# Four experts on one core: GpSimd's second parts of weights in pieces of 256 elements, and weight blocks split at other places of the program

## The chip, the core and the metric

The kernel runs on one core of a Trainium2 chip. The metric is the device time of one execution in microseconds (us). It was measured in three runs; one more execution was recorded by the hardware profiler, and all rows below come from that one.

The engines go by these names: PE multiplies matrices (TensorE; PEld is its loading of weights), DVE is VectorE, ACT is ScalarE, POOL is GpSimd, SP starts DMAs. SBUF is the memory on the chip, PSUM holds what PE writes. L1030 is line 1030 of the kernel before.

## What is computed

Attention over 2 x 8 heads (576 positions, a bias computed from distances), then a feed-forward layer with a rational activation, then a mixture of four experts. All is float32. The change lies in the experts alone:

```python
def _moe2_ref(x, domain_probs, w1, w2):      # x 1152 x 512, w1 4 x 512 x 1024, w2 4 x 1024 x 512
    p = domain_probs / (domain_probs.sum(-1, keepdims=True) + 1e-09)
    out = np.zeros((N, D), dtype=np.float32)
    for e in range(E):
        h = np.maximum(x @ w1[e], 0.0)
        out += p[:, e:e + 1] * (h @ w2[e])
    return out
```

## The kernel before

**Two parts per number.** PE multiplies float32 operands as a first part (the number rounded, made by an ACT copy) and a second part (number minus first part, made by a subtraction on DVE or POOL); each product is three matmuls: first x first, first x second, second x first. Activations are split as they come out of PSUM. Weights are loaded by SP into one of two `stage` buffers and split from there. A *split* below is ACT's copy followed by the subtraction.

**Two ways through the experts.** The 1152 tokens are three chunks of 384. One chunk goes the plain way, expert after expert (`expert_first`, four blocks f2 of first weights; then `expert_second`, three tiles t of 128 tokens, which need all four blocks of second weights). This is the *single part*; it ends at 531.66 us. The other two chunks, T1 and T2, then go together, again expert after expert: the *paired part*. There the two chunks and the two halves of the 512 inputs make a 2x2 block matrix, multiplied with 7 products in place of 8. For each of four groups g of an expert (`Square(e, g)`), product m (1 to 7) is 6 matmuls of 384 columns into one of three PSUM banks (`sa` for m = 1, 2; `sb` for 6, 5, 3; `sc` for 7, 4), and `gather(m)` has DVE and ACT add the products up in `part_sums`:

- m = 6: L1041 reads `sb` (after that m = 5 may add to it); m = 5: L1045 reads `sb` (after that m = 3 may), L1046 reads `sc`; m = 3: L1049; m = 4: L1052.
- Each finished quarter of h goes to `parts`: L1029 (ACT, first part with ReLU) and L1030 (DVE, second part). Three of four of these take h from `part_sums`, so both inputs of L1030 are in SBUF; the fourth takes it from `sa`, in PSUM.

The products run in this order: `(1 6 7 2 5)` of group 0, then for g = 1 to 3: `(1 6)` of g, `(3 4)` of g-1, `(7 2 5)` of g. That makes 26 products up to the last `5` of group 3, which I number 0 to 25; product 20 is m = 6 of group 3, product 21 is m = 3 of group 2. Then six tiles of `op` (`tile_products`) multiply h with the second weights. I call the 26 products the *squares* of an expert.

**Weights of the paired part.** A `Group` (G0 to G3 of each expert) holds one group's blocks `b` and their combinations `s`. It takes five steps: 0, ACT copies `b` (L400, L401); 1, DVE or POOL makes their second parts (L403, L404); 2, POOL makes the combinations in place in `stage` (L406 to L409, one after the other); 3, ACT copies them (L411); 4, DVE or POOL makes their second parts (L413). m = 1 needs steps 0 and 1, m = 6 needs all five. The second weights T0 to T3 (`WT`) are split in one step (L369, L370), on POOL.

**What sets the order.** Each engine works through its instructions in the order in which they are written. `order` lists the weight blocks in the order of their splitting; `turns(n)` does the next n steps of that list at its place in the program, and does nothing when the buffers' last readers are not yet written; `load_ahead` starts the load of the next block but one when a block is done. `side[0]` says who makes second parts of groups: DVE in the single part and beside the tiles, POOL beside the squares. `LAST_TURNS` and `TURNS` are the tables of places. `first` takes one of two PSUM buffers `hp`, so the product after next waits for ACT's L839 and DVE's L840 to have read it.

Of the kernel before, what the change touches and what calls it, by code (L numbers as in the profile page):

```python
# [15 lines left out]
ALU = mybir.AluOpType  # L16
# [5 lines left out]
E, FE = 4, 1024  # L22
# [25 lines left out]
def attention_then_two_ffn(ctx: ExitStack, tc: tile.TileContext, q, k, v, w1, b1, w2, w_in, w_out, ca, cb, probs, e_w1, e_w2, c_l, c_l8, c_p, c_x, out):  # L48
    nc = tc.nc
    act, dve, pool, pe, sp = nc.scalar, nc.vector, nc.gpsimd, nc.tensor, nc.sync  # L50

    def f32(ap):
        return ap.bitcast(F32)
# [119 lines left out]
    def catch_up(calls):  # L173
        now, calls[:] = calls[:], []
        for f in now:
            f()
# [150 lines left out]
    class Piece:  # L327
# [39 lines left out]
        def split(self):  # L367
            t = self.w.t[:, self.rows]
            act.activation(t[:, :, 0, :], self.raw, AF.Copy)  # L369
            self.w.eng.tensor_tensor(t[:, :, 1, :], self.raw, f32(t[:, :, 0, :]), ALU.subtract)  # L370

    class Group:
# [22 lines left out]
        def work(self, step, eng):  # L395

            b, s, raw = self.b, self.s, self.raw
            b11, b12, b21, b22 = (raw[:, i] for i in range(4))
            if step == 0:
                act.activation(b[:, 0, 0], b11, AF.Copy)  # L400
                act.activation(b[:, 2:4, 0], raw[:, 2:4], AF.Copy)  # L401
            if step == 1:
                eng.tensor_tensor(b[:, 0, 1], b11, f32(b[:, 0, 0]), ALU.subtract)  # L403
                eng.tensor_tensor(b[:, 2:4, 1], raw[:, 2:4], f32(b[:, 2:4, 0]), ALU.subtract)  # L404
            if step == 2:
                pool.tensor_tensor(b11, b12, b11, ALU.subtract)  # L406
                pool.tensor_tensor(b12, b22, b12, ALU.subtract)
                pool.tensor_tensor(b22, b22, b11, ALU.subtract)
                pool.tensor_tensor(b21, b21, b22, ALU.subtract)  # L409
            if step == 3:  # L410
                act.activation(s[:, :, 0], raw, AF.Copy)  # L411
            if step == 4:
                eng.tensor_tensor(s[:, :, 1], raw, f32(s[:, :, 0]), ALU.subtract)  # L413

    W1 = [(Weight(w_in, f2, False), Weight(w_out, f2, True)) for f2 in range(DFF // 256)]
    W2 = [[(Weight(e_w1[e], f2, False, 1), Weight(e_w2[e], f2, True, 1)) for f2 in range(FE // 256)] for e in range(E)]
# [1 line left out]
    order = [W1[f2][second] for grp in GROUPS for second in range(2) for f2 in grp]  # L418
    for e in range(E):
        order += [p[0] for p in W2[e]] + [p[1] for p in W2[e]]  # L420
    WS = [[Group(e_w1[e], g) for g in range(4)] for e in range(E)]
    WT = [[Weight(e_w2[e], f2, True, 1, pool) for f2 in range(FE // 256)] for e in range(E)]
    for e in range(E):
        order += WS[e][:3] + WT[e][:2] + WS[e][3:] + WT[e][2:]
    S_SLOT, T_SLOT = W_SLOT[3:5], W_SLOT[5]
    WO = W_SLOT * 3 + W_SLOT[:3] + (W_SLOT[6:] + W_SLOT[:3]) * E

# [11 lines left out]
    def can_convert():  # L439

        if state["done"] == len(order):
            return False
        return all(x not in holder or holder[x].left == 0 for x in order[state["done"]].slots())

    def convert(steps=5):

        for _ in range(steps):
            if state["step"] == 0 and not can_convert():
                return
            i = state["done"]  # L450
            if isinstance(order[i], Group):
                if state["step"] == 0:
                    order[i].place()
                order[i].work(state["step"], side[0])
                state["step"] = (state["step"] + 1) % 5
                if state["step"] == 0:
                    under_way.pop(i)
                    state["done"] += 1
                    load_ahead()
            elif state["step"] < 4:  # L460
                under_way[i].narrow(state["step"])
                state["step"] += 1
            else:
                order[i].place()
                under_way.pop(i).split()
                state["step"] = 0
                state["done"] += 1
                load_ahead()
# [224 lines left out]
    for i in range(-2, len(units)):  # L693
        if i + 2 < len(units):
            n, u = units[i + 2]
# [5 lines left out]
        if 0 <= i + 1 < len(units):  # L701
            n, u = units[i + 1]
            pair[n].exp(u)
        if i >= 0:
            n, u = units[i]
# [3 lines left out]
    def ready(w):  # L709
        while state["done"] <= order.index(w):  # L710
            assert state["step"] or can_convert()
            convert(5 - state["step"])
        return w.t
# [122 lines left out]
    def expert_first(u, f2):  # L836
        h = first(W2[u][f2][0], CHUNKS[0])
        hi, lo = tmp("h_hi", F32R), tmp("h_lo", F32R)
        act.activation(hi, h, AF.Relu)  # L839
        dve.scalar_tensor_tensor(out=lo, in0=h, scalar=0.0, in1=f32(hi), op0=ALU.max, op1=ALU.subtract)  # L840
        h_of[u, f2] = hi, lo
# [3 lines left out]
    for i in range(1, len(units) + LAG):  # L845
        on = i < len(units)
        if on:
            c, f2 = units[i]
# [70 lines left out]
    def turns(n):  # L919

        for _ in range(n):
            if state["done"] < len(order) and state["step"] == 0 and isinstance(order[state["done"]], Weight) and can_convert():
                state["step"] = 4
            convert(1)
# [28 lines left out]
    for i, a in enumerate((acc_01[:, 0], acc_01[:, 1], acc_2[:, 0])):  # L953
        acc_of[CHN // P * CHUNKS[0] + i] = a

    LAST_TURNS = 1, 1, 2, 3, 2, 3
    for u in range(E):
        for f2 in range(1, 4):
            if (u, f2) != (0, 1):
                expert_first(u, f2)  # L960
            turns(LAST_TURNS[f2 - 1] if u == E - 1 else 2 - f2 // 2 + ((u, f2) == (0, 2)))
            if 0 < u < E - 1 and results:
                results.pop(0)()
        if u + 1 < E:
            expert_first(u + 1, 0)
        for t in range(3):
            expert_second(u, t)
            if (u, t) == (E - 2, 0):
                assert not results
                making = sums_of_x()  # L970
            if (u, t) in ((E - 2, 0), (E - 1, 0), (E - 1, 1)):
                next(making)
            turns(LAST_TURNS[3 + t] if u == E - 1 else 1 + (t == 2))

    ffn.close()
    psum.close()
# [2 lines left out]
    def bank(tag):  # L979
        return ps.tile([P, 512], F32, tag=tag, name=tag)  # L980
# [12 lines left out]
    class Square:  # L993
# [13 lines left out]
        def __call__(self, *which):  # L1007

            for m in which:
                if m == 1:  # L1010
                    self.begin()
                k, x = RIGHT[m], LEFT[m]
                bank = self.bank[{1: 0, 2: 0, 3: 1, 5: 1, 6: 1, 4: 2, 7: 2}[m]]
                i = 0
                for c in range(2):
                    for wpart, xpart in ((0, 0), (0, 1), (1, 0)):
                        pe.matmul(bank, lhsT=self.w.t[k[0]][:, k[1], wpart, c], rhs=x[c][:, xpart], start=i == 0 and m in (1, 6, 7), stop=i == 5, skip_group_check=True)  # L1017
                        i += 1
                if m == 4:
                    self.w.left = 0  # L1020
                side[0] = pool
                waiting = self.gather(m)
                catch_up(later)
                later.extend(waiting)
                turns((self.g, m) in TURNS[self.e > 0])

        def parts(self, v, t):
            def f():
# [24 lines left out]
                return self.parts(u2, h21)  # L1053
            return []

    TURNS = [(0, 1), (0, 6), (0, 5), (1, 1), (1, 6), (0, 4), (1, 7), (1, 2), (1, 5), (1, 4), (2, 7), (2, 5), (3, 5)], [(0, 6), (0, 5), (0, 4), (1, 7), (1, 2), (1, 3), (1, 4), (2, 5), (3, 5)]
    for e in range(E):
        sq = [Square(e, g) for g in range(4)]
        sq[0](1, 6, 7, 2, 5)
        for g in range(1, 4):  # L1060
            sq[g](1, 6)
            sq[g - 1](3, 4)
            sq[g](7, 2, 5)

        tiles = [(c, t) for c in (T1, T2) for t in range(3)]
        ops = {}

        def tile_products(k, fs, begin, end):
            c, t = tiles[k]
            if begin:  # L1070
                ops[k] = bank("op")
            for x in (WT[e][f // 2] for f in fs):
                ready(x)
            j = CHN // P * c + t
            halves = (slice(0, DM),) if (e, k) != (E - 1, 5) else (slice(0, DM // 2), slice(DM // 2, DM))
            for cols in halves:
                second_products(ops[k][:, cols], lambda f, part: hs[f, c][:, part, t * P:(t + 1) * P], WT[e], fs, begin, end, cols)
                if end:
                    catch_up(later)
                    gathered(e, j, ops[k][:, cols], cols)  # L1080

        SOON, LATE = (0, 4, 1, 5, 2, 6), (3, 7)
        tile_products(0, SOON, True, False)
        sq[3](3, 4)
        catch_up(later)
        tile_products(1, SOON, True, False)
        for k in range(6):
            tile_products(k, LATE if k < 2 else SOON + LATE, k > 1, True)
            if k == 5:
                for x in WT[e]:  # L1090
                    x.left = 0
            side[0] = dve
            turns(2 if k < 2 else 3)


# [40 lines left out]
```

## Time and profile before

| | us |
|---|---|
| runs: median of 3 (lowest, highest) | 813.6 (811.23, 815.51) |
| profiled execution, its own time | 815.37 |
| its span, first to last instruction | 813.5 |
| PE busy | 771.0 (95% of the span) |
| DVE busy | 568.0 (70%) |
| ACT busy | 427.4 (53%) |
| POOL busy | 251.7 (31%) |
| paired part, 531.66 to the end | 281.9 |

The busy shares are means over stages. The single part keeps PE busy without a gap from 425 to 531.66 us; the gaps of the paired part lie in the squares. In timeline rows, `x6` merges six instructions, and what stands in brackets is the engine's idle time ahead of the row and who ended it. "PEclk" is the clock that was granted to TensorE, as a share of its full speed.

### The profile page before, as it was taken

How to read it: one execution, taken by the hardware profiler on the slowest of the kernel's cores; microseconds unless marked ns; L12 is line 12 of the kernel's file. 1: busy time of each engine (PE TensorE's matmuls, PEld its weight loads, DVE VectorE, ACT ScalarE, POOL GpSimd, SP SyncE). 2: the span in 40 equal slices, each digit the busy share in tenths (PEclk: the TensorE clock that was granted, in tenths of full speed). 3: DMA queues.
4: the chain of work that ended last, by engine and by line, in shares of the span. 5: the costliest groups of instructions: out<-in, count | busy, mean ns of one | idle time of the engine just before them, and what ended most of it. 6: DMA issues, size and time to landing. Idle time of an engine off the chain costs nothing.

```text
span 813.5 us, 15824 instructions
## 1 busy us (share of the span) xinstructions
PE 771.0 (95%) x6470; PEld 664.6 (82%) x6470; DVE 568.0 (70%) x868; ACT 427.4 (53%) x689; POOL 251.7 (31%) x207
## 2 busy tenths in 40 slices
PE   8998999988999999999999999987998998899898
PEld 5445666657999999999999898887887888888787
DVE  7989789996999999998754465457437436643831
ACT  6987567655988888787533352425224213322410
POOL 0000225432445466431100000166246145334510
PEclk9999999999999999999999999999999999999999
DMA  8898685640332133311143352223022112212101
GB/s 151 191 227 191 144 212 117 145 112 2 104 104 105 56 100 103 104 38 67 53 130 128 106 164 100 69 95 104 27 69 89 51 52 79 76 28 78 52 27 52
DMA packets 83945, 79.41 MB, mean 98 GB/s; under 512 B 38016, under 2 KB 62976, under 8 KB 83200
## 3 DMA queue, kind: packets, MB, share of 16 engines
q1 hardware_dynamic: 83440, 78.39, 35.2%
q8 instruction: 51, 0.84, 0.4%
q14 instruction: 22, 0.18, 0.1%
q10 hardware_dynamic: 432, 0.01, 0.0%
HBM read 59.20 MB, written 2.36 MB: 76 GB/s over the span
## 4 chain that ended last, share of the span: by engine, by line
PE 43%; DVE 24%; issue 11%; POOL 10%; ACT 8%; DMA 3%; SPq 1%; POOLq 0%; DVEq 0%; ACTq 0%
PE op L56 15%; PE hp L56 10%; PE sc L56 4%; PE o L568 4%; DVE hid L221 3%; DVE narrow L365 2%; DVE narrow L363 2%; DVE h L1030 2%; DVE qd L758 2%; PE yp L56 2%; PE sb L1017 2%; POOL w L370 2%; PE sc L1017 2%; DVE u L759 2%; DMA stage<-in_moe_w_dram 2%
## 5 line engine op out<-in xcount | busy, mean ns | idle before, releaser
L56 PE MATMUL hp<-x,wi 128*128 128x384 f32 x888 | 159.6, 337 | 2.8 <-DVE u L769 2.5
L56 PEld LDWEIGHTS hp<-x,wi 128*128 128x128 f32 x888 | 153.9, 188 | 5.6 <-issue 2.6
L56 PE MATMUL op<-w,h 128*128 128x512 f32 (+1 forms) x600 | 133.1, 382 | 0.6 <-DVE acc L888 0.6
L56 PEld LDWEIGHTS op<-w,h 128*128 128x128 f32 x600 | 109.5, 188 | 22.4 <-DVE acc L888 0.8
L56 PE MATMUL yp<-g_hi,w 128*128 128x384 f32 x384 | 102.1, 336 | 0.4 <-ACT y L824 0.4
L888 DVE SCALAR_TENSOR_TENSOR acc<-op,pr_sb,acc 128x512 f32<-128x512 f32 (+1 forms) x28 | 20.5, 731 | 82.3 <-PE op L56 82.3
L56 PEld LDWEIGHTS yp<-g_hi,w 128*128 128x128 f32 x384 | 69.7, 188 | 1.3 <-ACT y L824 0.7
L528 ACT ACTIVATE pq<-pq,nm 128x576 f32<-128x576 f32 x72 | 55.4, 771 | 21.3 <-DVE nm L519 20.9
L749 POOL TENSOR_TENSOR g_lo<-u,g_hi 128x768 fp32r<-128x768 f32 x24 | 45.3, 1887 | 62.9 <-ACT g_hi L748 51.5
L411 ACT ACTIVATE wi<-stage 128x1024 fp32r<-128x1024 f32 x16 | 17.0, 1061 | 90.5 <-POOL stage L409 90.5
L56 PE MATMUL yp<-g_lo,w 128*128 128x384 f32 x192 | 64.2, 335 | 0.0
L369 ACT ACTIVATE w<-stage 128x1024 fp32r<-128x1024 f32 x32 | 33.7, 1055 | 56.9 <-DMA stage<-in_moe_w_dram 56.8
L519 DVE CUSTOM_DVE_ANT_0 pq<-sc,ba 128x576 f32<-128x576 f32 x72 | 51.5, 746 | 16.4 <-PE sc L56 16.2
L56 PE MATMUL sc<-ks,qs 64*128 64x288 f32 (+1 forms) x320 | 57.6, 435 | 5.3 <-DVE nm L519 4.6
L1030 DVE SCALAR_TENSOR_TENSOR h<-part_sums,h 128x384 fp32r<-128x384 f32 x48 | 53.3, 1117 | 13.4 <-ACT h L1029 10.7
L56 PE MATMUL op<-w,h_hi 128*128 128x512 f32 x192 | 59.2, 389 | 0.0
L370 POOL TENSOR_TENSOR w<-stage,w 128x1024 fp32r<-128x1024 f32 x16 | 41.2, 2577 | 52.2 <-ACT w L369 52.2
L1029 ACT ACTIVATE h<-part_sums 128x384 fp32r<-128x384 f32 x48 | 24.7, 521 | 60.8 <-DVE part_sums L1049 35.0
L568 PE MATMUL o<-pt,val 32*64 32x160 f32 (+1 forms) x2304 | 49.2, 297 | 3.6 <-issue 2.4
L535 DVE STREAM_TRANSPOSE pt<-pq 128x576 f32<-128x576 f32 x72 | 52.4, 754 | 0.1
L568 PEld LDWEIGHTS o<-pt,val 32*64 32x64 f32 x2304 | 39.7, 132 | 13.8 <-issue 6.1
L232 PE MATMUL bps<-hid,wb 128*32 128x288 f32 x576 | 46.9, 410 | 2.9 <-DVE hid L221 2.0
(143 smaller groups left out, 1445.9 us busy)
## 6 DMA issues: line engine op xcount, KB each, us to landing
stage<-in_moe_w_dram SPq DMA_DIRECT2D x48, 512.0 KB, 3.5
ba<-ev SPq DMA_DIRECT2D x32, 288.0 KB, 5.2
words<-in_moe_w_in_dram SPq DMA_DIRECT2D x8, 1024.0 KB, 5.5
words<-in_moe_w_out_dram SPq DMA_DIRECT2D x8, 1024.0 KB, 5.0
stage<-in_moe_w_dram SPq DMA_DIRECT2D x64, 128.0 KB, 2.4
val<-val SPq DMA_DIRECT2D x21, 288.0 KB, 4.0
val<-in_v_dram SPq DMA_DIRECT2D x11, 288.0 KB, 4.1
out_dram<-acc SPq DMA_DIRECT2D x8, 256.0 KB, 2.0
```

Source lines behind the costliest of these rows:

```text
L56: pe.matmul(o, lhsT=l, rhs=r, start=start, stop=stop)
L232: pe.matmul(sc[32 * par:32 * par + 32, hf, :288], lhsT=wb.rearrange("p r h -> p (r h)"), rhs=tiles[par][:, 288 * hf:288 * hf + 288], start ...
L369: act.activation(t[:, :, 0, :], self.raw, AF.Copy)
L370: self.w.eng.tensor_tensor(t[:, :, 1, :], self.raw, f32(t[:, :, 0, :]), ALU.subtract)
L519: dve.tensor_tensor_reduce(out=self.row(u + e).rearrange("p (a j) -> p a j", a=2), in0=o[:, :, :288], in1=bs.rearrange("p (a j) -> p a j", ...
L528: act.activation(self.row(u), self.row(u), AF.Exp, bias=least.pop((self.n, u)), scale=-1.0, accum_out=self.sm[:, u:u + 1])
L535: dve.transpose(self.pt[:, 5 * e + k], self.row(u))
L568: pe.matmul(self.o[64 * e:64 * e + 64, a, c:c + 32 * m], lhsT=val[self.n % 2][r, NKB * e + b], rhs=self.pt[r, i:i + m, 32 * b:32 * b + 32] ...
L749: pool.tensor_tensor(lo, u, f32(hi), ALU.subtract)
L1017: pe.matmul(bank, lhsT=self.w.t[k[0]][:, k[1], wpart, c], rhs=x[c][:, xpart], start=i == 0 and m in (1, 6, 7), stop=i == 5, skip_group_che ...
L1029: act.activation(t[:, 0], v, AF.Relu)
L1030: dve.scalar_tensor_tensor(out=t[:, 1], in0=v, scalar=0.0, in1=f32(t[:, 0]), op0=ALU.max, op1=ALU.subtract)
```

## The change

The subtractions of POOL are cut into pieces of 256 elements: the second weights' L370 (1024 elements) becomes four instructions on L373, a group's step 1 three (on DVE too, which had two), step 4 four on POOL and one on DVE as before. Steps move to other places. Line numbers after the change are higher by 5 (L370 is L375) to 8 (L888 is L896; L413 is L420).

```diff
         def split(self):
             t = self.w.t[:, self.rows]
             act.activation(t[:, :, 0, :], self.raw, AF.Copy)
+            if self.w.eng is pool and not self.w.w64:
+                for i in range(4):
+                    x = slice(i // 2, i // 2 + 1), slice(256 * (i % 2), 256 * (i % 2) + 256)
+                    pool.tensor_tensor(t[:, x[0], 1, x[1]], self.raw[:, x[0], x[1]], f32(t[:, x[0], 0, x[1]]), ALU.subtract)
+                return
             self.w.eng.tensor_tensor(t[:, :, 1, :], self.raw, f32(t[:, :, 0, :]), ALU.subtract)
...
         def work(self, step, eng):
+            n = 4 if eng is dve else 1
...
             if step == 1:
-                eng.tensor_tensor(b[:, 0, 1], b11, f32(b[:, 0, 0]), ALU.subtract)
-                eng.tensor_tensor(b[:, 2:4, 1], raw[:, 2:4], f32(b[:, 2:4, 0]), ALU.subtract)
+                for i in (0, 2, 3):
+                    eng.tensor_tensor(b[:, i, 1], raw[:, i], f32(b[:, i, 0]), ALU.subtract)
...
             if step == 4:
-                eng.tensor_tensor(s[:, :, 1], raw, f32(s[:, :, 0]), ALU.subtract)
+                for i in range(0, 4, n):
+                    eng.tensor_tensor(s[:, i:i + n, 1], raw[:, i:i + n], f32(s[:, i:i + n, 0]), ALU.subtract)
...
+    order.insert(-1, WS[0][0])
     for e in range(E):
-        order += WS[e][:3] + WT[e][:2] + WS[e][3:] + WT[e][2:]
+        order += WS[e][e == 0:3] + WT[e][:2] + WS[e][3:] + WT[e][2:]
...
-    LAST_TURNS = 1, 1, 2, 3, 2, 3
+    PACE = {0: (2, 2, 1, 1, 1, 2), 1: (2, 1, 1, 1, 1, 2), 2: (2, 1, 1, 3, 3, 3), 3: (2, 2, 2, 2, 1, 2)}
...
-                turns((self.g, m) in TURNS[self.e > 0])
+                turns((self.g, m) in TURNS)
...
-    TURNS = [(0, 1), (0, 6), (0, 5), (1, 1), (1, 6), (0, 4), (1, 7), (1, 2), (1, 5), (1, 4), (2, 7), (2, 5), (3, 5)], [(0, 6), (0, 5), (0, 4), (1, 7), (1, 2), (1, 3), (1, 4), (2, 5), (3, 5)]
+    TURNS = (0, 6), (0, 3), (1, 7), (1, 2), (1, 5), (1, 4), (2, 7), (2, 5), (3, 5)
...
-            turns(2 if k < 2 else 3)
+            turns(3 if k in (2, 3, 4) else 2)
```

Worked through, the tables give these places (the steps of a group in brackets; B0 to B3 are the second weights of single experts):

| place | before | after |
|---|---|---|
| single part, experts 0 and 1 | | the same |
| single, expert 2, behind tiles 0, 1, 2 | last first weight; B0 of expert 3; B1, B2 | last first weight, B0, B1; B2, G0 (0, 1); G0 (2, 3, 4) |
| single, expert 3, behind f2 = 1, 2, 3 | B3; G0 (0); G0 (1, 2) | B3, G1 (0); G1 (1, 2); G1 (3, 4) |
| single, expert 3, behind tiles 0, 1, 2 | G0 (3, 4), G1 (0); G1 (1, 2); G1 (3, 4), G2 (0) | G2 (0, 1); G2 (2); G2 (3, 4) |
| squares of expert 0, up to product 8 | G2 (1 to 4), T0, T1 | T0 behind product 1, T1 behind 7 |
| tile 5 of experts 0 to 2 | G2 (3, 4), T0 of the next | G2 (3, 4) of the next |
| squares of experts 1 to 3 | T1 behind product 1; G3 (0) behind 8, (1, 2) behind 9, 10, (3) behind 14, (4) behind 15 | T0 behind 1, T1 behind 7; G3 (0, 1, 2) behind 9, 10, 11, (3) behind 15, (4) behind 16 |
| T2, T3 of the squares | behind products 18, 25 | the same |

**ACT, from the last weights of the single part's expert 2 to expert 3's third h.** `w` is a block of second weights, `wi` a group's block, `hp` the PSUM buffer of `expert_first`. Before:

```order
L369 ACTIVATE w<-stage 128x2x512 x3
L839 ACTIVATE h_hi<-hp 128x768
L369 ACTIVATE w<-stage 128x2x512
L839 ACTIVATE h_hi<-hp 128x768
L400 ACTIVATE wi<-stage 128x256
L401 ACTIVATE wi<-stage 128x2x256
L839 ACTIVATE h_hi<-hp 128x768
```

After:

```order
L369 ACTIVATE w<-stage 128x2x512 x3
L406 ACTIVATE wi<-stage 128x256
L407 ACTIVATE wi<-stage 128x2x256
L417 ACTIVATE wi<-stage 128x4x256
L847 ACTIVATE h_hi<-hp 128x768
L369 ACTIVATE w<-stage 128x2x512
L406 ACTIVATE wi<-stage 128x256
L407 ACTIVATE wi<-stage 128x2x256
L847 ACTIVATE h_hi<-hp 128x768 x2
```

The whole ACT side of G0 now stands ahead of expert 3's second h (`h_hi<-hp`, f2 = 1), and G1's first copies ahead of its third.

**DVE, the same stretch.** `L936` to `L939` prepare sums of x for the paired part; `L888` adds a tile to the result. Before:

```order
L936 TENSOR_TENSOR yacc<-yacc 128x2x384
L938 TENSOR_TENSOR yacc<-yacc 128x2x384
L939 TENSOR_TENSOR yacc<-yacc 128x2x384
L370 TENSOR_TENSOR wi<-stage,wi 128x4x256
L888 SCALAR_TENSOR_TENSOR acc<-op,pr_sb,acc 128x512
L370 TENSOR_TENSOR w<-stage,w 128x2x512
L888 SCALAR_TENSOR_TENSOR acc<-op,pr_sb,acc 128x512
L370 TENSOR_TENSOR w<-stage,w 128x2x512 x2
L840 SCALAR_TENSOR_TENSOR h_lo<-hp,h_hi 128x768
```

After:

```order
L375 TENSOR_TENSOR wi<-stage,wi 128x4x256
L375 TENSOR_TENSOR w<-stage,w 128x2x512 x2
L896 SCALAR_TENSOR_TENSOR acc<-op,pr_sb,acc 128x512
L375 TENSOR_TENSOR w<-stage,w 128x2x512
L410 TENSOR_TENSOR wi<-stage,wi 128x256 x3
L896 SCALAR_TENSOR_TENSOR acc<-op,pr_sb,acc 128x512
L420 TENSOR_TENSOR wi<-stage,wi 128x4x256
L848 SCALAR_TENSOR_TENSOR h_lo<-hp,h_hi 128x768
```

Two blocks of second weights are split ahead of the first L896 here, and steps 1 and 4 of G0 stand ahead of the `h_lo` of expert 3's second h.

**POOL, the squares of expert 1.** `stage<-stage` is step 2 of G3. Before:

```order
L370 TENSOR_TENSOR w<-stage,w 128x2x512 x2
L403 TENSOR_TENSOR wi<-stage,wi 128x256
L404 TENSOR_TENSOR wi<-stage,wi 128x2x256
L406 TENSOR_TENSOR stage<-stage 128x256
L407 TENSOR_TENSOR stage<-stage 128x256
L408 TENSOR_TENSOR stage<-stage 128x256
L409 TENSOR_TENSOR stage<-stage 128x256
L413 TENSOR_TENSOR wi<-stage,wi 128x4x256
```

After:

```order
L373 TENSOR_TENSOR w<-stage,w 128x256 x8
L410 TENSOR_TENSOR wi<-stage,wi 128x256 x3
L412 TENSOR_TENSOR stage<-stage 128x256
L413 TENSOR_TENSOR stage<-stage 128x256
L414 TENSOR_TENSOR stage<-stage 128x256
L415 TENSOR_TENSOR stage<-stage 128x256
L420 TENSOR_TENSOR wi<-stage,wi 128x256 x4
```

The order is the same; 9 instructions have become 19, none over 256 elements.

## Rows read from the trace of the kernel before

**Rows 1.** Stretches: squares of experts 0 to 3, busy us by engine, granted clock

```profile
531.66:568.58 36.92, 29.66 (x157) 28.46 (x156) 23.53 (x31) 15.86 (x28) 27.12 (x21) 0.95 0.30 93
603.50:636.84 33.34, 29.45 (x158) 28.49 (x157) 22.92 (x30) 13.27 (x25) 15.78 (x10) 0.95 0.26 80
671.75:705.59 33.84, 29.45 (x158) 28.49 (x156) 22.91 (x30) 13.28 (x25) 15.76 (x10) 0.95 0.24 78
740.50:774.29 33.79, 29.35 (x158) 28.38 (x156) 23.00 (x30) 13.27 (x25) 15.76 (x10) 0.95 0.20 63
```

**Rows 2.** Waits in the paired part: who waited for whom, us, times, longest

```profile
PE sb L1017 <- DVE part_sums L1045: 12.8, 7, 2.9
```

**Rows 3.** PE's timeline, expert 1: start us, us, instructions, [idle ahead <- releaser]

```profile
603.50 1.21 PE L1017 MATMUL sa<-x,wi 128*128 128x384 f32 x6
604.54 1.20 PE L1017 MATMUL sb<-s,wi 128*128 128x384 f32 x6
...
626.42 1.21 PE L1017 MATMUL sb<-s,wi 128*128 128x384 f32 x6
629.96 1.62 PE L1017 MATMUL sb<-x,wi 128*128 128x384 f32 x6 [2.33 <-DVE part_sums L1045]
...
634.75 1.20 PE L1017 MATMUL sa<-x,wi 128*128 128x384 f32 x6
```

**Rows 4.** The stretch behind that wait; the eighth column is the granted clock

```profile
629.96:633.30 3.34, 3.34 (x12) 3.34 (x13) 2.49 (x5) 1.05 (x2) 0.00 (x0) 0.62 0.54 157
```

**Rows 5.** Timeline of POOL and DVE ahead of that wait

```profile
623.95 2.42 POOL L413 TENSOR_TENSOR wi<-stage,wi 128x1024 fp32r<-128x1024 f32 x1 [1.17 <-ACT wi L411]
626.30 2.71 POOL L370 TENSOR_TENSOR w<-stage,w 128x1024 fp32r<-128x1024 f32 x1
...
624.31 5.12 DVE L1030 SCALAR_TENSOR_TENSOR h<-part_sums,h 128x384 fp32r<-128x384 f32 x2 [0.75 <-ACT h L1029]
```

**Rows 6.** Line L1030: its two forms, ns min/median/max, first and last start

```profile
L1030 DVE SCALAR_TENSOR_TENSOR h<-part_sums,h x48: 548/560/2730, 544.4 to 781.9; 128x384 fp32r<-128x384 f32 x48
L1030 DVE SCALAR_TENSOR_TENSOR h<-sa,h x16: 547/548/558, 542.0 to 775.6; 128x384 fp32r<-128x384 f32 x16
```

**Rows 7.** Timeline of POOL and DVE, expert 0, pieces of 256 elements

```profile
557.01 0.75 POOL L408 TENSOR_TENSOR stage<-stage 128x256 f32<-128x256 f32 x1
557.84 0.94 POOL L409 TENSOR_TENSOR stage<-stage 128x256 f32<-128x256 f32 x1
...
557.03 1.14 DVE L1030 SCALAR_TENSOR_TENSOR h<-part_sums,h 128x384 fp32r<-128x384 f32 x1
```

**Rows 8.** POOL's timeline, expert 1: end of group 3's step 1, start of step 2

```profile
617.83 1.30 POOL L404 TENSOR_TENSOR wi<-stage,wi 128x512 fp32r<-128x512 f32 x1
619.08 1.04 POOL L406 TENSOR_TENSOR stage<-stage 128x256 f32<-128x256 f32 x1
```

**Rows 9.** Timeline, expert 1: DVE at the start of the squares

```profile
604.37 1.21 DVE L413 TENSOR_TENSOR wi<-stage,wi 128x1024 fp32r<-128x1024 f32 x1
...
609.49 0.56 DVE L1046 TENSOR_TENSOR part_sums<-sc,part_sums 128x384 f32<-128x384 f32 x1
```

**Rows 10.** Timeline, single part, between experts 2 and 3: PE, DVE, ACT

```profile
502.81 12.65 PE L56 MATMUL hp<-x,wi 128*128 128x384 f32 x72
...
497.56 1.22 DVE L370 TENSOR_TENSOR wi<-stage,wi 128x1024 fp32r<-128x1024 f32 x1
...
508.01 0.96 DVE L840 SCALAR_TENSOR_TENSOR h_lo<-hp,h_hi 128x768 fp32r<-128x768 f32 x1 [1.43 <-ACT h_hi L839]
...
502.02 1.06 ACT L369 ACTIVATE w<-stage 128x1024 fp32r<-128x1024 f32 x1 [11.36 <-DMA stage<-in_moe_w_dram]
...
507.17 0.81 ACT L839 ACTIVATE h_hi<-hp 128x768 fp32r<-128x768 f32 x1 [1.84 <-PE hp L56]
```

**Rows 11.** Timeline, expert 0: a group's four loads, and ACT's second copy of them

```profile
548.81 1.90 SPq L393 DMA_DIRECT2D stage<-in_moe_w_dram  x4
...
553.03 0.63 ACT L401 ACTIVATE wi<-stage 128x512 fp32r<-128x512 f32 x1 [1.39 <-DMA stage<-in_moe_w_dram]
```

More of the change, by code (lines that the diff above doesn't have):

```diff
@@ L960, in attention_then_two_ffn @@
                 expert_first(u, f2)
-            turns(LAST_TURNS[f2 - 1] if u == E - 1 else 2 - f2 // 2 + ((u, f2) == (0, 2)))
+            turns(PACE.get(u, PACE[1])[f2 - 1])
             if 0 < u < E - 1 and results:
@@ L972, in attention_then_two_ffn @@
                 next(making)
-            turns(LAST_TURNS[3 + t] if u == E - 1 else 1 + (t == 2))
+            turns(PACE.get(u, PACE[1])[3 + t])
     ffn.close()
```

## Prediction, made before the changed kernel had run

> **What bounds the kernel now.** First the stretches of the four squares [rows 1]: PE is idle 3.9 to 7.3 us in each, its granted clock has a mean of 0.95, and each lasts 33.3 to 36.9 us. The time that PE alone needs is read from its timeline [rows 3]: product 0 starts at 603.50, product 1 at 604.54, so a product is 1.04 us and 26 of them 27.04 us. The squares together last 36.92 + 33.34 + 33.84 + 33.79 = 137.9 us against 4 x 27.04 = 108.2 us: **29.7 us** is all that the paired part can give back. PE is the engine that ends everything else, so each microsecond of it counts in full.
>
> Who takes them? In the waits of the paired part PE's longest entry is DVE's L1045, 12.8 us in seven waits [rows 2]. One of the seven is in rows 3: product 21 starts at 629.96 after 2.33 us of idleness. Ahead of it [rows 5] stand two L1030 that take 5.12 us together, while L1030 alone takes 0.55 us; they begin under POOL's L413 (623.95 to 626.37) and end just behind POOL's L370 (626.30 to 629.01). L1030's two forms tell why [rows 6]: with h from PSUM it takes 547 to 558 ns in all 16 cases, with both inputs in SBUF 548 to 2730. So a DVE instruction with two inputs in SBUF stands still until POOL's current instruction is over, and POOL's instructions of 1024 elements are 2.4 us long. L1045 is queued behind it on DVE, and PE waits for L1045.
>
> An idle PE costs a second time. Behind the 2.33 us the granted clock was 0.62 in the mean over 3.34 us [rows 4], that is mostly at the lower of its two levels (1.2 GHz), and three products took 634.75 - 629.96 = 4.79 us in place of 3.12 [rows 3]: **1.7 us** more. All four squares have a mean of 0.95 [rows 1]; 5% of 33.34 us is the same 1.7 us.
>
> **The pieces.** What does DVE gain? Rows 7 have pieces of 256 elements with an L1030 beside them: L408 runs from 557.01 to 557.76, L1030 starts at 557.03 and ends at 558.17, 0.41 us behind L408; L409 starts at 557.84 and takes 0.94 us in place of 0.75. The waiting DVE instruction thus gets its turn between two pieces, loses some 0.6 us, and costs POOL some 0.2 us. With pieces, L1030 takes 0.55 to 1.3 us and two of them at most 2.6 in place of 5.1. Is that enough? The two L1030 ahead of an L1045 can begin when m = 4 of the group before is done, and PE needs L1045 before product m = 3, five products or 5.2 us later; L1052, two L1030 and L1045 take 0.55 + 2.6 + 0.55 = 3.7 us. I book the waits for L1041 and L1045 at nothing.
>
> What do pieces cost POOL? A piece alone takes 0.75 us [rows 7]. Pieces that depend on each other start 0.83 us apart (557.01, 557.84); where nothing depends, the next starts before the last is over (L404 ends at 619.13, L406 stands at 619.08 [rows 8]), so the new ones should be 0.70 apart. 512 elements take 1.30 us [rows 8] and 1024 take 2.42 [rows 5], so four pieces are 2.8 to 3.3 us, 0.4 to 0.9 more. POOL is not full, so this matters in one place.
>
> **The third wait.** Product 20 (m = 6 of group 3) needs all five steps of G3. Before, POOL ended G3's L413 at 626.37 and product 20 started at 626.42 [rows 3, 5]: just in time, on a PE that was already 2.1 us late. After, T0 and T1 stand ahead of G3 on POOL, and all is in pieces. From product 0 as zero: L1046 ends at 6.55 (609.49 + 0.56 - 603.50 [rows 9]), ACT copies h (384 elements, 0.5 by the 0.63 for 512 [rows 11] and the 1.06 for 1024 [rows 10]) and T1 (1.06), so T1's pieces start at 8.2. T1 is there by then: its load begins when G2's step 4 ends, at 2.1 [rows 9], and takes 3.2 (below). Then four pieces with two L1030 between them (2.8 to 3.3, + 0.5), three pieces of step 1 (2.1 to 2.5), step 2 (4 x 0.83, + 0.25), ACT's copy (1.06 + 0.1), four pieces of step 4 (2.8 to 3.3, + 0.25). The sum is 21.4 to 22.8. PE reaches product 20 at 20 x 1.04 = 20.8. So **PE waits 0.6 to 2.0 us there**; I take 1.0, since the pieces are nearest to L404 and L406, which follow each other without a gap. Steps 0 are no limit: G3's load starts when T0 is done on POOL (near 6), its four parts take 4.2 us (below), and ACT comes to it only behind L1052 of product 8, which ends at 9.4. Squares then take 27.04 + 1.0 + 0.2 for the small starts = 28.25 us, four times 113.0: a **gain of 24.9 us**. Expert 0 gains most, 8.7 us: its G2 no longer stands in the squares, where it held ACT up.
>
> The price of a piece is where the Trainium skill says otherwise. The page "GPSIMD Engine Reference", section "Performance versus the Vector engine", gives 2.6 cycles for an element and 4497 ns for 2048; at the 1.2 GHz of its specifications that leaves some 60 ns for an instruction itself, an estimate, and 0.61 us for a piece. The same section's two software hops for each instruction speak against cutting up, but by its figures they are cheap. By them the 11 pieces of this chain would end 1 us earlier and product 20 would not wait at all; the sum would be 790 in place of 794. The trace's own piece of 0.75 us is nearer to what runs here, so it is used.
>
> **A new wait between experts 2 and 3.** The order on ACT and DVE puts all of G0 ahead of the reading of expert 3's second `hp`. PE needs that buffer again for its fourth product: the three stand in one row from 502.81 [rows 10], 24 matmuls or 4.16 us each, so at 511.13. Now the chain. The last first weight's L370 can't move forward, since it stands behind the sums of x; it ends at 498.78 [rows 10]. That frees the stage buffer for B1, and ACT begins B1 at 502.02, waiting for its DMA [rows 10]: 3.2 us. ACT 1.06, DVE 1.22: 504.35 frees the buffer for G0. A group's load takes 4.2 us from its start to ACT's second copy (548.81 to 553.03 [rows 11]): 508.6. Then ACT 0.63, two pieces on DVE 0.75, POOL's last two combinations 1.6, ACT's copy of the combinations 1.06, with handovers 512.7. Only then ACT copies the waiting h (0.81), and DVE, done with G0's step 4 (1.22), makes its second part (0.96) [rows 10]: 514.9. **PE waits 3.7 us**, in a stage that had no gap, and I add 1.7 us of low clock: a **loss of 5.4 us**. Behind it ACT waits for G1's load as well, but what it holds up is not due before the thirteenth matmul of the next tile. The bounds are 0 (the loads land 4 us sooner) and 5.4.
>
> **Edits at nothing.** DVE's step 1 in three pieces costs 0.1 us each, hidden beside tiles in which DVE is idle more than half. The first parts of experts 0 and 1 do not move. T3's pieces: its product needs only its first two, and these end 1.4 us after their start where the whole took 2.4. Should a T come late, PE would wait in the tiles, which are now without a gap.
>
> **Sum.** On the profiled execution: 815.4 - 24.9 + 5.4 = 795.9 us. It is 1.8 us above the median of the runs, so against the median: 813.6 - 19.5 = **794.1**.
>
> **Rivals.**
> 1. *Closer to the ideal.* No wait between the experts, or none at product 20: -4.0 or -5.4 or both, 784.7 to 790. For it: the page's price of a piece. Against it: two DMA landings from rows that do not change.
> 2. *POOL is later still.* Pieces 0.83 apart and the low clock behind each wait at product 20: (2.0 - 1.0 + 1.7) x 4 = 10.8 more, 799 to 805. For it: gaps of 2.3 us did end in a low clock. Against it: they were longer than 2.0.
> 3. *Slower.* DVE does not get its turn between pieces that are queued back to back, but only behind the last of four. Then experts 1 to 3 stay as they are, each critical pair of POOL's is 0.9 us longer (3.6 in four), expert 0 gains its G2 alone (-2.7), and the wait between the experts comes on top (+5.4): 819.9. The point is the second piece: if L1030 waits for two or more on average, the gain is gone. Against it: rows 7, where the turn changed in the middle of a chain. For it: that chain's pieces depend on each other, the new ones do not. The Trainium skill's page "SBUF — State Buffer", section "Who interferes with whom", has the first starter hold the port for its whole instruction and does not say who is next when both stand in line; no row here shows it for independent pieces of 256.
> 4. *Little change.* DVE is freed, but ACT, which waits in order for POOL's step 2 ahead of the next h, becomes the limit: 808 to 815. Against it: that copy is due 2 us before PE needs what is behind it.
>
> **How the numbers follow.** About 0.5% (4 us) is what a measurement of this kernel can tell from no change. Forecast (790 to 799): 0.60. Rival 1: 0.14. Rival 2: 0.17. Rival 3: 0.03. Rival 4: 0.06, of which 0.01 lies below 809.5. So faster 0.92, same 0.05, slower 0.03. The range takes in the forecast and rivals 1 and 2, whose ends are the bounds of the unknown prices: 785 to 805.
>
> **What would show it.** L1030 with both inputs in SBUF: longest near 1.3 us, mean under 0.9 (1117 ns now). PE's waits for L1045 and L1041 gone from the list; a wait of PE for POOL's L420 at product 20 in each expert, 0.6 to 2.0 us. A wait of PE near 511 us for DVE's L848, about 3.7 us, in a stage that had none, and a low clock behind it. Squares of 28 to 29 us in all four experts. The prediction is wrong if L1030 still takes over 2 us under pieces (rival 3), if squares stay over 31 us, or if PE runs through from 502 to 531 us.

## Result and the profile after

| | before | after |
|---|---|---|
| median of 4 runs each (lowest, highest), us | 814.4 (811.2, 815.5) | 792.3 (790.8, 792.9) |
| ratio, 95% interval | | 0.973 (0.970 to 0.976) |
| profiled execution, its own time | 815.4 | 792.6 |
| four squares | 137.9 | 111.4 |
| paired part starts at | 531.66 | 535.37 |

The change is faster by 2.7%. (A fourth run of before has made its median 814.4.) The forecast was 794.1, range 785 to 805. The size was right; the experiments show that what the forecast had booked on the pieces came from the places.

The four squares after, as [rows 1]: length, then busy times of PE, PEld, DVE, ACT, POOL, and the granted clock:

```profile
535.37:563.22 27.85, 27.33 (x157) 27.01 (x156) 19.04 (x33) 13.24 (x24) 17.97 (x23) 1.00 0.31 101
598.14:625.99 27.85, 27.33 (x157) 27.01 (x156) 18.17 (x30) 13.58 (x25) 17.98 (x23) 1.00 0.28 92
660.90:688.76 27.86, 27.34 (x158) 27.01 (x156) 18.17 (x30) 13.59 (x25) 17.98 (x23) 1.00 0.30 92
723.67:751.52 27.85, 27.33 (x157) 27.01 (x156) 18.18 (x30) 13.58 (x25) 17.98 (x23) 1.00 0.24 76
```

All four are alike, at a clock of 1.00 where it was 0.95. PE's waits of the whole run that bear on the change: for L1053 (L1045 of before [rows 2]) and L1049 (L1041 of before) there is none left; L420 has four, one for each expert; L848 has one.

```profile
PE hp L56 <- DVE h_lo L848: 3.6, 1, 3.6
...
PE sb L1025 <- POOL wi L420: 2.1, 4, 0.5
```

L1038, which is L1030 of [rows 6], has lost its long cases: 1101 ns at most where it was 2730.

```profile
L1038 DVE SCALAR_TENSOR_TENSOR h<-part_sums,h x48: 548/559/1101, 542.7 to 759.1; 128x384 fp32r<-128x384 f32 x48
L1038 DVE SCALAR_TENSOR_TENSOR h<-sa,h x16: 547/548/549, 541.8 to 752.8; 128x384 fp32r<-128x384 f32 x16
```

Product 20 of expert 1 on PE, then POOL (T0's pieces, and the chain that product 20 waits for: T1's pieces, group 3's steps 1 and 4), then two L1038 that DVE does beside T1's pieces:

```profile
618.94 0.51 PE L1025 MATMUL sb<-s,wi 128*128 128x384 f32 x2
619.97 0.97 PE L1025 MATMUL sb<-s,wi 128*128 128x384 f32 x4 [0.52 <-POOL wi L420]
```

```profile
600.95 2.86 POOL L373 TENSOR_TENSOR w<-stage,w 128x256 fp32r<-128x256 f32 x4 [3.58 <-ACT w L369]
606.51 3.17 POOL L373 TENSOR_TENSOR w<-stage,w 128x256 fp32r<-128x256 f32 x4 [2.70 <-ACT w L369]
609.65 2.45 POOL L410 TENSOR_TENSOR wi<-stage,wi 128x256 fp32r<-128x256 f32 x3
...
616.77 3.15 POOL L420 TENSOR_TENSOR wi<-stage,wi 128x256 fp32r<-128x256 f32 x4 [1.17 <-ACT wi L417]
```

```profile
608.17 1.92 DVE L1038 SCALAR_TENSOR_TENSOR h<-part_sums,h 128x384 fp32r<-128x384 f32 x2
```

The chain ends 21.78 us behind product 0 (598.14), 1.0 behind the start of product 20. PE loses only 0.52 of it, because the product's first two matmuls need only first parts of the weights.

The seam between experts 2 and 3, as [rows 10]: PE, then ACT, then DVE.

```profile
501.08 8.49 PE L56 MATMUL hp<-x,wi 128*128 128x384 f32 x48
513.17 1.13 PE L56 MATMUL hp<-x,wi 128*128 128x384 f32 x4 [3.60 <-DVE h_lo L848]
```

```profile
506.71 0.63 ACT L407 ACTIVATE wi<-stage 128x512 fp32r<-128x512 f32 x1 [1.31 <-DMA stage<-in_moe_w_dram]
509.93 1.06 ACT L417 ACTIVATE wi<-stage 128x1024 fp32r<-128x1024 f32 x1 [2.59 <-POOL stage L415]
510.89 0.79 ACT L847 ACTIVATE h_hi<-hp 128x768 fp32r<-128x768 f32 x1
```

```profile
511.02 1.23 DVE L420 TENSOR_TENSOR wi<-stage,wi 128x1024 fp32r<-128x1024 f32 x1 [2.18 <-ACT wi L417]
512.16 0.95 DVE L848 SCALAR_TENSOR_TENSOR h_lo<-hp,h_hi 128x768 fp32r<-128x768 f32 x1
```

PE ends its second product at 509.57, waits 3.60 us, and takes 5.83 us from 513.17 to 519.00 for the 24 matmuls that take 4.16 in [rows 10]; the granted clock of that stretch is 0.71:

```profile
513.17:519.00 5.83, 5.83 (x24) 5.83 (x25) 2.47 (x4) 1.75 (x3) 0.00 (x0) 0.71 0.63 180
```

That is 3.60 + 1.67 = 5.3 us. The balance of the profiled executions: squares -26.5, seam +5.3, and -1.7 from the stages that the change does not touch (the single part's row of 502.81 [rows 10] starts at 501.08). Most of this last goes with a low clock between 170 and 190 us (0.91), which the execution of before had and this one (1.00) had not. Before, then after:

```profile
170.00:190.00 20.00, 17.32 (x381) 13.12 (x370) 15.03 (x30) 7.82 (x21) 9.62 (x13) 0.91 0.38 100
```

```profile
170.00:190.00 20.00, 17.62 (x450) 14.04 (x438) 15.21 (x32) 9.26 (x22) 10.04 (x14) 1.00 0.40 102
```

The sum is -22.9, the times differ by 22.8.

### The profile page after: what moved, and what is told of

It is laid out like the page before. It is cut to its first block, busy times and chain, and to the rows that moved or that the text cites. A ratio compares the mean times of both kernels' runs of the same rounds, so it can differ in the third digit from the quotient of the medians.

```text
span 790.8 us, 15912 instructions
## 1 busy us (share of the span) xinstructions
PE 762.3 (96%) x6470; PEld 659.3 (83%) x6470; DVE 558.0 (71%) x883; ACT 429.3 (54%) x689; POOL 255.2 (32%) x268
## 5 line engine op out<-in xcount | busy, mean ns | idle before, releaser
L56 PE MATMUL hp<-x,wi 128*128 128x384 f32 x888 | 161.4, 339 | 6.4 <-DVE h_lo L848 3.6
L56 PEld LDWEIGHTS hp<-x,wi 128*128 128x128 f32 x888 | 155.5, 190 | 9.5 <-DVE h_lo L848 3.9
L896 DVE SCALAR_TENSOR_TENSOR acc<-op,pr_sb,acc 128x512 f32<-128x512 f32 (+1 forms) x28 | 20.4, 730 | 73.9 <-PE op L56 73.9
L527 DVE CUSTOM_DVE_ANT_0 pq<-sc,ba 128x576 f32<-128x576 f32 x72 | 51.4, 745 | 16.2 <-PE sc L56 16.1
L373 POOL TENSOR_TENSOR w<-stage,w 128x256 fp32r<-128x256 f32 x64 | 48.1, 782 | 40.0 <-ACT w L369 40.0
L576 PE MATMUL o<-pt,val 32*64 32x128 f32 (+1 forms) x2304 | 48.9, 293 | 2.6 <-issue 1.4
L1037 ACT ACTIVATE h<-part_sums 128x384 fp32r<-128x384 f32 x48 | 25.1, 522 | 46.2 <-DVE part_sums L1057 36.9
L56 PEld LDWEIGHTS sc<-ks,qs 64*128 64x128 f32 (+1 forms) x320 | 29.8, 175 | 23.2 <-DVE nm L527 10.2
```

What stands on the lines that cost most here:

```text
L56: pe.matmul(o, lhsT=l, rhs=r, start=start, stop=stop)
L373: pool.tensor_tensor(t[:, x[0], 1, x[1]], self.raw[:, x[0], x[1]], f32(t[:, x[0], 0, x[1]]), ALU.subtract)
L527: dve.tensor_tensor_reduce(out=self.row(u + e).rearrange("p (a j) -> p a j", a=2), in0=o[:, :, :288], in1=bs.rearrange("p (a j) -> p a j", ...
L576: pe.matmul(self.o[64 * e:64 * e + 64, a, c:c + 32 * m], lhsT=val[self.n % 2][r, NKB * e + b], rhs=self.pt[r, i:i + m, 32 * b:32 * b + 32] ...
L896: dve.scalar_tensor_tensor(out=a, in0=op, scalar=pr_sb[:, j, e:e + 1], in1=a, op0=ALU.mult, op1=ALU.add)
L1037: act.activation(t[:, 0], v, AF.Relu)
```

## Experiments

All are compared with the kernel before on their own chip; a square runs from product 0 to the first tile. Line numbers differ by a few: L1030 (before, runs 3 and 4), L1031 (run 2), L1037 (runs 1 and 5) and L1038 (after) are one instruction; step 4 of a group is L413 (before, runs 2 to 4 and 9), L418 (run 10) or L420 (after, runs 1, 5 and 6).

| kernel | squares, experts 0 / 1 / 2 / 3 | wait at seam | median | ratio (95%) |
|---|---|---|---|---|
| before | 36.92 / 33.34 / 33.84 / 33.79 | none | 814.4 | |
| after | 27.85 / 27.85 / 27.86 / 27.85 | 3.6 | 792.3 | 0.973 (0.970 to 0.976) |
| 1 pieces only | 40.48 / 30.10 / 30.16 / 30.09 | none | 809.0 | 0.995 (0.992 to 0.997) |
| 2 places only | 27.04 / 27.04 / 27.04 / 27.04 | 3.5 | 790.8 | 0.972 (0.970 to 0.975) |
| 3 T0's and T1's places only | 37.44 / 30.84 / 29.25 / 29.25 | none | 803.1 | 0.987 (0.982 to 0.991) |
| 4 group 3's place only | 36.84 / 29.59 / 29.96 / 30.10 | none | 802.2 | 0.987 (0.984 to 0.990) |
| 5 as 3, and pieces | 41.23 / 28.15 / 28.15 / 28.15 | none | 804.5 | 0.989 (0.986 to 0.992) |
| 6 after, T1 earlier | 27.32 / 27.40 / 27.40 / 27.52 | 3.6 | 793.4 | 0.975 (0.972 to 0.978) |
| 7 after, seam moved | 28.92 / 27.85 / 27.84 / 27.84 | none | 789.5 | 0.971 (0.968 to 0.975) |
| 8 places, seam moved, G2 on POOL | 32.63 / 27.05 / 27.05 / 27.05 | none | 791.1 | 0.973 (0.970 to 0.976) |
| 9 places, seam moved | 31.38 / 27.04 / 27.04 / 27.05 | none | 789.9 | 0.971 (0.969 to 0.974) |
| 10 as 9, expert 0's T0 in pieces | 28.71 / 27.04 / 27.04 / 27.04 | none | 784.9 | 0.967 (0.964 to 0.970) |
| 11 after, on the chip of 10 | 27.85 / 27.86 / 27.85 / 27.85 | 3.7 | 793.8 | 0.976 (0.974 to 0.979) |

**1 and 2: the two halves of the change apart.** Run 1 has the pieces in `split` and `work` and the tables of before; run 2 the tables of after and whole instructions.

> GpSimd's second parts in pieces of 256, but the blocks split at the positions of the kernel before. Theory A (the pieces carry the gain, since VectorE then waits for 0.75 us instead of 2.4): L1030 with two SBUF inputs at most 1.3 us, squares of experts 1 to 3 at 27.5 to 28.5 us each, expert 0, which still has group 2 in its squares, 28 to 33; no wait at the seam between experts 2 and 3; 788 to 796 us. Theory B (the places carry it, since in the new order L1038 hardly ever meets GpSimd): squares of experts 1 to 3 stay above 31 us, over 803 us.

> The new positions with whole GpSimd instructions of 1024 elements. Theory A: VectorE's instruction with two SBUF inputs is up to 2.7 us long again, PE waits for VectorE behind it, squares 31 to 33 us each, the seam costs its 5.4 us as in the kernel after; 804 to 814 us. Theory B: squares 27.9 to 29 us, 790 to 797 us.

Theory A, which was the prediction's for experts 1 to 3, falls; B's answer, that the places carry the gain, holds. Its lengths do not: run 1's squares of experts 1 to 3 are 30.1 to 30.2 us where A had 27.5 to 28.5 and B over 31, and run 2's are shorter than B's 27.9. With the places alone no square has a wait of PE: 27.04 us is PE's own time. The pieces alone take 3.2 to 3.7 us off experts 1 to 3. In expert 1 PE's waits for DVE shrink from 3.90 us (0.61 for L1041, 0.96 and 2.33 for L1045) to 0.73 (0.33 and 0.40), and 1.23 for POOL's pieces at product 20 come in. On expert 0 the pieces alone put 3.6 us. PE is idle there for 7.9 us where it was 7.3 [rows 1]; the rest goes with a granted clock of 0.87 where it was 0.95:

```profile
531.97:572.45 40.48, 32.57 (x157) 31.29 (x156) 19.63 (x32) 15.88 (x28) 30.16 (x38) 0.87 0.26 85
```

In the new places the pieces cost 0.8 us for each expert (27.85 against 27.04); the medians of run 2 and after, 790.8 and 792.3, are too close to show it.

Yet the pieces did to DVE what was said. Run 1, DVE and ACT of expert 1:

```profile
628.33 1.81 DVE L1037 SCALAR_TENSOR_TENSOR h<-part_sums,h 128x384 fp32r<-128x384 f32 x2 [1.57 <-ACT h L1036]
```

```profile
616.05 1.06 ACT L369 ACTIVATE w<-stage 128x1024 fp32r<-128x1024 f32 x1 [6.88 <-DMA stage<-in_moe_w_dram]
617.01 0.47 ACT L1036 ACTIVATE h<-sa 128x384 fp32r<-128x384 f32 x1
```

The pair that took 5.12 us in [rows 5] takes 1.81. But ACT stands 6.88 us for T1's load, with h behind it. A row like it stands in the trace of before, and the prediction had made nothing of it. ACT in expert 1 there, with all that the next two runs turn on:

```profile
611.20 1.06 ACT L369 ACTIVATE w<-stage 128x1024 fp32r<-128x1024 f32 x1 [5.84 <-DMA stage<-in_moe_w_dram]
612.17 0.47 ACT L1029 ACTIVATE h<-sa 128x384 fp32r<-128x384 f32 x1
...
622.81 1.06 ACT L411 ACTIVATE wi<-stage 128x1024 fp32r<-128x1024 f32 x1 [1.65 <-POOL stage L409]
623.77 0.92 ACT L1029 ACTIVATE h<-part_sums 128x384 fp32r<-128x384 f32 x2
```

Two places on ACT: T1's copy waits for its DMA 5.84 us with copies of h and `part_sums` behind it; and group 3's step 3 waits 1.65 us for POOL's combinations with two copies of h behind it. These then come together, and their two L1030 run into POOL's L413 and L370. T1's load was late too: SP started it at 607.89, 4.4 us after product 0, behind POOL's second part of T0; after, where T0 stands behind product 1, it starts at 600.25, 2.1 us after product 0, behind group 2's last step. SP's longest wait around there, before and after:

```profile
SPq L343 <- POOL w L370: 8.9, 1, 8.9
```

```profile
SPq L343 <- DVE wi L420: 9.8, 1, 9.8
```

**3 and 4: which place?** Experts 1 to 3 of the kernel before, whole instructions; run 3 also leaves T0 to the squares.

```diff
-[(0, 6), (0, 5), (0, 4), (1, 7), (1, 2), (1, 3), (1, 4), (2, 5), (3, 5)]
+[(0, 6), (0, 3), (0, 4), (1, 7), (1, 2), (1, 3), (1, 4), (2, 5), (3, 5)]
...
-            turns(2 if k < 2 else 3)
+            turns(3 if k in (2, 3, 4) else 2)
```

> The kernel before (whole GpSimd instructions, no change at the seam, expert 0 as it was) with only T0 and T1 of experts 1 to 3 moved: T0 from the last tile to product 1, T1 from product 1 to product 7; the steps of group 3 stay. Theory C (what cost experts 1 to 3 their time is ScalarE standing still for 5.8 us for T1's DMA with the copies of h queued behind it; L1030 then came late and in pairs under GpSimd's long instructions): no wait of ScalarE for a DMA in the squares, PE's waits for L1041 and L1045 go, squares of experts 1 to 3 27.0 to 27.6 us, expert 0 as before, 795 us against 813.6. Rival D (group 3's steps, with ScalarE's step 3 ahead of two copies of h, carry it): the wait of 2.3 us stays, squares 30 to 32 us, 803 to 808 us.

And run 4:

```diff
-[(0, 6), (0, 5), (0, 4), (1, 7), (1, 2), (1, 3), (1, 4), (2, 5), (3, 5)]
+[(0, 6), (1, 7), (1, 2), (1, 5), (1, 4), (2, 7), (2, 5), (3, 5)]
```

> The kernel before with only the steps of group 3 of experts 1 to 3 moved to their new places, one product later each (step 4 two); T0 and T1 stay. Theory C: ScalarE still stands for T1's DMA, the two early waits (0.6 to 1.2 and 0.96 us) stay, squares 29 to 32 us, 801 to 809 us. Rival D: the wait of 2.3 us for L1045 goes and with it the low clock, squares 28.6 us, 798 us.

Each theory has half. With T1 moved, ACT no longer waits for it and the two early waits go, but the pair stays. Run 3, ACT, DVE and PE:

```profile
623.10 1.06 ACT L411 ACTIVATE wi<-stage 128x1024 fp32r<-128x1024 f32 x1 [2.18 <-POOL stage L409]
624.07 0.92 ACT L1029 ACTIVATE h<-part_sums 128x384 fp32r<-128x384 f32 x2
```

```profile
624.61 5.13 DVE L1030 SCALAR_TENSOR_TENSOR h<-part_sums,h 128x384 fp32r<-128x384 f32 x2 [0.91 <-ACT h L1029]
```

PE still waits 1.92 to 1.95 us for L1045 there (expert 1, at 30.84 us, also has a granted clock of 0.94; expert 2, at 29.25, has 1.00). With group 3 moved (run 4), one h is copied ahead of step 3 and both waits for L1045 are gone, also the early one of 0.96 us, which theory C had put down to T1; those for L1041 stay (0.60, 0.98, 1.12 us), and POOL, late behind T1, makes PE wait 1.18 us at product 20:

```profile
614.25 1.31 PE L1017 MATMUL sb<-s,wi 128*128 128x384 f32 x6 [0.60 <-DVE part_sums L1041]
625.40 0.97 PE L1017 MATMUL sb<-s,wi 128*128 128x384 f32 x4 [1.18 <-POOL wi L413]
```

Both moves together stand in run 2, beside those of the single part and of expert 0. There DVE still meets a whole L413, but with one L1031 and not two, and has no one waiting:

```profile
617.82 2.46 DVE L1031 SCALAR_TENSOR_TENSOR h<-part_sums,h 128x384 fp32r<-128x384 f32 x1 [0.45 <-ACT h L1030]
```

**5: do pieces stand in for the second move?** Run 1 with run 3's table.

> The old positions with pieces, and only T0 and T1 of experts 1 to 3 at their new positions. If the two causes are separate (ScalarE's wait for T1's DMA makes the early waits; two copies of h behind step 3, then two L1037 under two GpSimd instructions make the third), pieces cure the third as moving step 3 does, and T1's position the first two: squares of experts 1 to 3 27.0 to 27.9 us, 791 to 794 us if expert 0 stays at 40.5 us. If pieces do not replace the move of step 3, a wait of about 1 us or more for L1052 or for GpSimd stays in each of them, 29 us or more, 797 to 801 us.

Nearly: 28.15 us, with one wait of 0.83 us, for POOL's pieces of L420 at product 20 and none for DVE. The time expected was wrong by its own base: run 1's 809.0 less three times 2 us is 803, and 804.5 came. Expert 0 of the old places stays at 41 us.

**6: the wait at product 20.**

```diff
-    TURNS = (0, 6), (0, 3), (1, 7), (1, 2), (1, 5), (1, 4), (2, 7), (2, 5), (3, 5)
+    TURNS = (0, 6), (0, 5), (0, 4), (1, 2), (1, 5), (1, 4), (2, 7), (2, 5), (3, 5)
```

> The kernel after with T1 split three products earlier (behind product 4 instead of 7) and group 3's step 0 behind product 8 instead of 9. Theory (product 20 waits 0.52 us in each expert because GpSimd's chain from T1 to group 3's step 4 ends 0.5 us late): the chain starts 1.5 us earlier, limited then by group 3's load, the four waits vanish, squares 27.3 us, 790.2 us. Rival (the chain is set by group 3's load, or ScalarE's copy of T1 now holds up h): the wait stays or moves to another bank, 791.5 to 793 us.

By the trace the theory holds: three of the four waits are gone, one of 0.20 is left, and the squares are 0.3 to 0.5 shorter. The time can't show 1.8 us in all: the profiled execution reached the paired part 4.0 us later than that of after (539.40 against 535.37), with granted clocks of 0.98 (100 to 170 us) and 0.96 (170 to 210 us) where after had 1.00, and the intervals overlap.

**7 to 11: the seam, and a better version.** Group 0's five steps go behind the reading of expert 3's second `hp`:

```diff
-    PACE = {0: (2, 2, 1, 1, 1, 2), 1: (2, 1, 1, 1, 1, 2), 2: (2, 1, 1, 3, 3, 3), 3: (2, 2, 2, 2, 1, 2)}
+    PACE = {0: (2, 2, 1, 1, 1, 2), 1: (2, 1, 1, 1, 1, 2), 2: (2, 1, 1, 3, 1, 0), 3: (5, 3, 3, 2, 1, 2)}
```

> The kernel after with the five steps of expert 0's paired group 0 placed behind the reading of expert 3's second first-layer product instead of ahead of it; all later blocks return to their places by expert 3's second-layer products. Theory (VectorE's h_lo stands behind group 0, and this costs 3.6 us of wait and 1.7 to 1.8 us of low clock): the wait for L848 is gone, no stretch of low clock, the paired part starts 5.4 us earlier, 787 us. Rival (group 0 now comes later than its product or holds up the next h): a wait of the same size appears at the next h or at the start of the paired part, 790 to 793 us.

The wait and the low clock are gone (PE's three products run through in 12.65 us, as before), and the paired part starts 5.9 us earlier than after. 1.07 us come back in expert 0: DVE is later relative to PE, and L1049 makes it wait 0.78. The median gained 2.9 us, not 5.3, with runs from 787.0 to 791.8.

Run 8: whole instructions, and group 2's step 4 of expert 0 on POOL behind product 0. Run 9: whole instructions with the table above.

> The new positions with whole GpSimd instructions, group 0 of expert 0 behind the reading of expert 3's second first-layer product, and group 2's step 4 on GpSimd behind product 0 instead of on VectorE behind the sums of x. Expected of all theories so far: no wait at the seam, squares 27.04 to 27.3 us, 5.3 us below the positions alone: 785.5 us, below both kernels.

> The new positions with whole GpSimd instructions, and at the seam the turns of the run with group 0 behind the reading of expert 3's second first-layer product; group 2's step 4 stays on VectorE ahead of the squares (in the run before it stood on GpSimd there, and VectorE's last two second parts of the sums of x took 5.41 us under GpSimd's long instructions). Expected: no wait at the seam (-5.3 us against the positions alone), squares of experts 1 to 3 27.05 us, expert 0 some 1 us longer by a wait of 0.8 us for L1042; 786.5 us. If VectorE again stands behind a long GpSimd instruction at product 5 of expert 0, that square is 30 us or more and the time 789 to 791 us.

Both missed, at one spot: in expert 0 DVE's last two-input instructions ahead of product 4 come under whole POOL instructions. In run 8 two second parts of the sums of x (1.02 us otherwise) take 5.41, in run 9 group 2's step 4 (1.23 otherwise) takes 3.17; PE waits 3.73 and 2.48 us behind them. The gain at the seam is spent there. Here, then, pieces are what is needed. Run 10 is run 9 with them in one block alone:

```diff
+            if self.w is WT[0][0]:
+                for i in range(4):
...
+                return
```

> The run with whole GpSimd instructions and the moved seam, and of all second parts on GpSimd only those of expert 0's T0 in pieces of 256. In the run before it VectorE's group 2 step 4 took 3.17 us in place of 1.22 under the whole instruction of that T0, and PE waited 2.5 us for L1042 behind it and lost 1.9 us to the low clock. Expected: that step 1.2 to 1.9 us, the wait of PE 0.8 us as in the run with pieces and the moved seam, expert 0's square 28.1 us, the other three 27.05 us; 3.2 us below the run before, 786.7 us in the median, and 5 to 6 us below the kernel after on the same chip. If pieces of T0 alone do not free VectorE there, the square stays above 30 us.

> The kernel after once more, on the chip of the mixed run, to compare the two: squares 27.85 us each, the seam with its wait of 3.6 us, 792 us.

The step on DVE in runs 9 and 10:

```profile
535.18 3.17 DVE L413 TENSOR_TENSOR wi<-stage,wi 128x1024 fp32r<-128x1024 f32 x1
```

```profile
533.64 1.52 DVE L418 TENSOR_TENSOR wi<-stage,wi 128x1024 fp32r<-128x1024 f32 x1
```

Expert 0's square falls from 31.38 to 28.71 us, the wait to 1.32 (expected: 28.1 and 0.8). Run 10 has 784.9 us against 793.8 of the kernel after on the same chip; their ratios' intervals (0.964 to 0.970, 0.974 to 0.979) are apart. It beats both kernels.

## Why the prediction was right, and where it was not

- **What bounds the kernel: half right.** The squares, PE's waits and the low clock behind them were where the time went, and all but 3.2 us of the 29.7 came back. But "Who takes them?" was answered from DVE's side alone; what ACT stood waiting for in the squares has no part in the answer.
- **The pieces: the mechanism right, the worth wrong.** DVE does get its turn between independent pieces (1101 ns at most, 1.3 expected), so rival 3 is out: the pairs of L1037 take 1.81 us. The step that failed is "I book the waits for L1041 and L1045 at nothing", as an effect of the pieces. They did go, but the places took them. With the pieces alone 0.7 us of these waits stay in each of experts 1 to 3 and 1.2 for POOL come in. Of the forecast gain of 24.9 us the working put 8.7 down to a place, that of expert 0's G2, and 16.2 to pieces in experts 1 to 3; there pieces alone gain 10.6 and places alone 19.9. Over all four squares it is 7.1 and 29.7. That the sum came out all the same is partly luck: the places, made in the same change, gave more than was booked on the pieces, and the pieces cost 3.2 us of it. The working weighed what the moved steps cost on POOL, and not what they had held up on ACT. The two causes, T1's copy (moved with T0) and group 3's step 3 ahead of two copies of h, took 2.5 to 4.6 and 3.7 to 3.9 us off each of experts 1 to 3 when moved alone (runs 3 and 4).
- **The third wait: chain right, loss half.** Expected 21.4 to 22.8 us behind product 0, measured 21.78; taken as 1.0 of wait, 0.52 in fact (first parts come first). A square is 27.85, expected 28.25: the gain is 26.5 and not 24.9. Without pieces the chain ends at 20.36 (run 2: 619.87 - 599.51) and nobody waits. T0's four pieces take 2.86 us, 0.72 each; by the Trainium skill's page "GPSIMD Engine Reference", section "Performance versus the Vector engine", a piece was an estimate of 0.61. The measurement decides, as the prediction chose.
- **The new wait between experts 2 and 3: right.** 3.7 and 1.7 expected, 3.60 and 1.67 measured, and run 7 takes it away.
- **Edits at nothing:** the tiles stayed as they were; PE's list has one wait there, 0.6 us for L896 in the last tile, which before has too (L888).
- **The sum:** -24.9 + 5.4 against -26.5 + 5.3; the median's 22 us hold these and the early stages' clock.
- **Rival 4 (ACT as the limit)** named the right engine for the wrong kernel: by runs 3 and 4 ACT's order held DVE up before, and the change freed it.
- **Open:** expert 0's 9.1 us were not taken apart. Places alone give all of it (9.9), with group 2 out of its squares; which of its moves does so was not tried. The trace of before supports the prediction's reason, G2 holding ACT up, for the first of its three waits, 2.58 us for L1039, which stands on ACT behind G2's step 3:

```profile
535.23 1.06 ACT L411 ACTIVATE wi<-stage 128x1024 fp32r<-128x1024 f32 x1 [12.03 <-POOL stage L409]
...
537.01 0.47 ACT L1039 ACTIVATE part_sums<-sa 128x384 f32<-128x384 f32 x1
```

## What to carry to other kernels

A long wait for one engine often begins one engine earlier: ask what held up the instruction that came late, down to an instruction that waits for a DMA with others queued behind it. A step that waits, put one place later in an in-order queue, can be worth more than a faster step. Cut long instructions that shut another engine out only where that engine meets them with someone waiting; elsewhere the pieces cost their own time.

## What the runs showed of the hardware

- Which engine goes next when DVE's instruction with two SBUF inputs and POOL's next one both stand in line: DVE, also between POOL pieces that do not depend on each other (1101 ns at most of 48 in the kernel after, where one whole piece of 0.72 us and its own 0.55 would make 1.27). The Trainium skill's page "SBUF — State Buffer", section "Who interferes with whom", leaves it open; here is one pair of operations that shows it. Between whole instructions it goes first as well, but then takes up to 2.73 us [rows 6] in place of 0.55; a whole one of 2.42 us and its own 0.55 would make 2.97.
- Executions of one kernel differ by up to 7 us (run 10: 783.3 to 790.0), and some of it comes from stages far from the change: the granted clock between 100 and 210 us was below 1.00 in none, one or two stretches of a profiled execution (after: none; before: one; run 6: two), with the paired part 1.7 us later in before by the row of the seam and 4.0 us in run 6. Stage lengths show effects that the medians can't.
